# One batch's transposes moved from TensorE to VectorE, and half additions moved forward in the last group

## The chip, the cores and the metric

The kernel runs on one core of a Trainium2 chip. The metric is device time in microseconds (us), the median of three runs. The engines are TensorE (PE, and PEld for its weight loads), VectorE (DVE), ScalarE (ACT), GpSimd (POOL) and SyncE (SP). SP issues most DMAs and does no arithmetic; POOL issues the others. Each engine works through its instructions in the order in which they stand, and waits on semaphores for what the other engines and the DMAs deliver.

## The reference

An attention block on x (4 batches, 8 heads, 512 rows, 64 columns) and a small state (32 rows for each head) feeds two dense layers, one after the other.

```python
scores  = scale * x @ state.T;  a  = softmax(scores);   xread = a @ state
scores2 = scale * state @ x.T;  a2 = softmax(scores2);  sread = a2 @ x
x = concat([xread, sread]) as (4 * 544, 512)
h = x @ w_in;  x = (h - tanh(h)) @ w_out                       # layer 1, 512 -> 2048 -> 512
h = x @ w_in;  out = (h * tanh(softplus(h))) @ w_out           # layer 2, 512 -> 2048 -> 512
```

All of it is float32. Both kinds of scores need x with its 64 columns on the partitions, that is, x transposed.

## The kernel before

A float32 product is made of three passes: each operand is split into a high part (`gh`, `wh`, `ath`) and a remainder (`gl`, `wl`, `atl`), and PE adds high by high, remainder by high and high by remainder. ACT makes the high part, DVE subtracts it for the remainder. The names in the rows are these tiles.

Layer 1 is a sequence of steps, 16 for each batch and 4 for the state rows: steps 0 to 15 are batch 0, 16 to 31 batch 1, 32 to 47 batch 2, 48 to 51 the state rows, 52 to 67 batch 3. A step is an up product into the bank `h` (ACT takes its tanh, DVE subtracts, ACT and DVE split the result into `gh` and `gl`) and, a few steps later, a down product into four banks `acc0` to `acc3`. The four banks are shared by the batches: when a batch ends, ACT and DVE copy them out to `y`, and the next batch's first down product writes them again. Batch 2 begins with `acc3`.

Beside this, each step has side work in a table (`at(step, fn)`): the attention of the next batch, the products `swp` of the state with the weights, and background pieces (`run_piece`) that convert layer 2's weights (`st` tiles, loaded by SP, turned by ACT into `w` and `r`, joined and split by DVE, and stored by POOL as `wi` and `wo`). `keep_pace` decides how many pieces a step runs: it draws straight lines through the points in `pace` and runs pieces while fewer are done than the line says, at most three or four in a step, and only while ten slots of the tile store are free (`RESERVE`).

Batch 2's x is transposed by DVE: `load_xq` brings x in 32 DMAs of 32 KB, in pieces of 128 bytes, so that transposing 32 by 32 blocks (`xt_q`, STREAM_TRANSPOSE) gives what is wanted. The x of the other batches is loaded by `load_x` in rows of 1 KB, transposed by PE in four 128 by 128 products into a side bank (`xtp`), and copied out to `xt`. For batch 3 this stands in the steps 35, 35, 36 and 37, and the scores in step 39. `at_sread` uses the tiles of `load_x` too.

Layer 2 runs in groups of seven products each (a form of Strassen's method). In the last two groups DVE also joins the halves of earlier results into `out` (`combos`: four additions of 256 columns in each of the four items `second(0)`, `second(1)`, `first(0)`, `first(1)`). They wait in the list `soon`, and `slot`, which runs after each of the seven products, takes one item from it. The last group's down products then go through three banks `acc` in turn, and DVE adds each into `out` before the bank is written again.

The lines that order the moved work:

```python
        v = u.t.rearrange("p (i g d) -> p i g d", i=2, g=8)          # load_xq
        V.transpose(out=XT[b, k].t, in_=u.t)                         # xt_q
            if soon and done[0] != 4:                                # slot, in group
                soon.popleft()()
        at(start[b - 1] + (8 if b == QUARTERS else -1), lambda b=b: load_x(b))
    pace = [(start[1] + 8, 0), (start["s"], 52), (start["2"], 96)]
```

All slots of the tile store come from one list (`get`, `put`); `newest` takes the slot that was given back last. The instruction order that results is made by a scheduler, within the dependencies.

Of the kernel before, what the change touches and what calls it, by code (L numbers as in the profile page):

```python
# [31 lines left out]
QUARTERS = 2  # L32
# [48 lines left out]
def attention_moe_kernel(  # L81
# [16 lines left out]
    KD = DM // 128  # L98
# [24 lines left out]
    def get(name, dtype=F32, newest=False, whole=False):  # L123
        if halves and dtype == F32 and not whole:
            return halves.popleft()
        i = free.pop() if newest else free.popleft()
        return Unit(slots.tile([128, 512], dtype, tag=f"k{i}", name=name), i)
# [311 lines left out]
    def load_xq(b, k):  # L439


        u = get("xq", whole=True)
        v = u.t.rearrange("p (i g d) -> p i g d", i=2, g=8)
        for i in range(2):
            src = x[b, 2 * k + i].rearrange("(l g e) (c d) -> (e c) l g d", g=8, e=2, c=2)
            for c in range(4):
                nc.sync.dma_start(out=v[c * 32:(c + 1) * 32, i], in_=src[c])
        P["q", b, k] = u
# [45 lines left out]
    def sc_c(b, i):  # L494
        SC[b, i] = get("scs")
        out = SC[b, i].t.rearrange("p (q e l h) -> p q e l h", q=2, e=2, h=4)
        for e in range(2):
            src = P["c", b][e][:, i * 256:(i + 1) * 256]
            if b == QUARTERS:
                src = src.rearrange("p (h q l) -> p q l h", h=4, q=2)  # L500
            else:
                src = src.rearrange("p (q l h) -> p q l h", q=2, h=4)
            evac(out[:, :, e], src, e if b else 1 - i)
# [127 lines left out]
        )  # L631

    def at_steps(b):
        turn = xt_q if b == QUARTERS else at_xt
        return [lambda k=k: turn(b, k) for k in range(KD)] + [
            lambda: at_scores(b),
            lambda: (at_exp(b, 0), at_exp_t(b, 0)),
            lambda: at_norm(b, 0),
            lambda: (at_exp(b, 1), at_exp_t(b, 1), at_read_t(b, 0)),
            lambda: at_norm(b, 1),  # L640
            lambda: at_read_t(b, 1),
            lambda: at_sread(b),
            lambda: at_sturn(b),
        ]
# [383 lines left out]
        V.tensor_tensor(out=o.t, in0=bank, in1=u.t, op=ALU.add)  # L1028
        return o

    def group(u, g, fill, ahead, with_s, rate, whole=False, keep=0, per=(), mid=None, end=None):


        a, b, c = (psum.tile([128, 512], F32, tag=t, name="h") for t in UB)
        whole_g[0] = g
        done = [0]
        more = rate + (rate > 1)

        def slot(pieces, *after):
            done[0] += 1  # L1040
            for _ in range(2 if done[0] - 1 in per else 1):
                if len(fill) > keep:
                    f = fill.popleft()
                    if f:
                        f()
            if soon and done[0] != 4:
                soon.popleft()()
            for f in after:
                f()
            for _ in range(1 if whole else 2):  # L1050
                if ahead:
                    ahead.popleft()()
            background(pieces, 0)

        def free_w(*xs):
            for x in xs:
                put(*(W2.pop((g, x, k)) for k in range(KH)))

        product(u, g, "m1", a, True)
        m1 = copy_of(a)  # L1060
        slot(more)
        product(u, g, "m6", b, True)
        p = plus(b, m1)
        slot(more)
        product(u, g, "m7", c, True)
        if with_s:
            hs = psum.tile([128, 512], F32, tag=SB_, name="hs")
            gs = s_up(g, hs)
        free_w("a1")
        slot(rate)  # L1070
        product(u, g, "m2", a, False)
        c11 = mish((0, 0), a, whole=whole)
        slot(0, lambda: mish_lo(*c11))
        if with_s:
            divide = s_turn(g, gs, hs)
        product(u, g, "m5", b, False)
        free_w("s12")
        q = plus(b, m1)
        background(1, 0)
        h22 = plus(c, q, q)  # L1080
        c22 = mish((1, 1), h22.t, h22, whole)
        slot(min(u + g, 1), lambda: mish_lo(*c22))
        product(u, g, "m3", b, False)
        free_w("s34")
        h12 = plus(b, m1, m1)
        c12 = mish((0, 1), h12.t, h12, whole)
        slot(rate, lambda: mish_lo(*c12), *([divide] if with_s else []), *([mid] if mid else []))
        product(u, g, "m4", c, False)
        free_w("a2")
        h21 = plus(c, p, p)  # L1090
        c21 = mish((1, 0), h21.t, h21, whole)
        slot(rate, lambda: mish_lo(*c21), *([end] if end else []))
        while len(fill) > keep or ahead:
            slot(rate)
# [84 lines left out]
    soon = deque()  # L1179
# [208 lines left out]
    def at(step, fn, back=None):  # L1388

        def held():  # L1390
            kept = [e.floor for e in engines]
            for e, m in zip(engines, marks[-back]):
                e.floor = m
            fn()
            for e, m in zip(engines, kept):
                e.floor = m

        side.setdefault(step, []).append(held if back else fn)

    seq = []  # L1400
    start = {}
# [27 lines left out]
                at(k + 5, lambda b=b: at_sturn(b), 1)  # L1429
    when = {2: (3, 4, 5, 7, 8, 9, 10, 11, 12, 13, 15, 16), 3: (3, 3, 4, 5, 7, 8, 9, 11, 12, 12, 13, 15)}  # L1430
    for b in (2, 3):
        if b == QUARTERS:
            for k in range(KD):
                at(start[b - 1] + when[b][k] - 3, lambda b=b, k=k: load_xq(b, k))
        at(start[b - 1] + (8 if b == QUARTERS else -1), lambda b=b: load_x(b))
        for i, f in zip(when[b], at_steps(b), strict=True):
            at(start[b - 1] + i, f)
    for b in (1, 2, 3):
        at(start[b] - (3 if b > 1 else 1), lambda b=b: at_a(b))
    at(start[3], lambda: bg.extend(pieces_y(0) + list(late)))  # L1440
    pace = [(start[1] + 8, 0), (start["s"], 52), (start["2"], 96)]
    done = [0]

    def keep_pace(i):
# [146 lines left out]
    for j, (u, g) in enumerate(groups):  # L1591
        n = j % len(ROUND2)
        plain = u == 0 or n >= WHOLE
        ahead = loads_out(g) if plain else deque()
        if j + 1 < len(groups):
            ahead += loads_in(groups[j + 1][1])
        if u and n == 0:
            background(len(bg), 0)
        if (u, n) == (0, 2):
            background(len(bg), 0)  # L1600
            send(now[0] + 1, 0)
            send(0, now[0] + 1)
            widen(stage.tile([128, 1024], F32, tag="st", name="wide") for _ in range(3))
            later = pieces_y(1)
            bg.extend(pieces_ys() + later[:EARLY])
        elif (u, n) == (0, last_g):
            bg.extend(later[EARLY:])
            load, steps = more_t(ROUND2[4])
            ahead.append(load)
        rate = 2 if n == last_g or u == 0 and n < 2 else 1  # L1610
        fill = list(fill)
        if u == 0:
            group(u, g, deque(fill), ahead, False, rate)
            fill = downs(u, g, False)
            continue
        if plain:
            if n == WHOLE:
                fill = deque(fill)
                early, closing = combos(2 * u)
                soon.extend([lambda: None, lambda: None, early])  # L1620
                group(u, g, fill, ahead, True, rate, keep=4, per=(0, 2, 4, 6))
                fill = list(fill) + downs(u, g, True)
            else:
                soon.extend(closing)
                first = fill[4:]
                fill = deque(fill[:4] + first[:2] + first[4:5] + first[2:4] + first[5:])
                group(u, g, fill, ahead, True, rate)
                fill = downs(u, g, True, True)
            continue
        if n == 0:  # L1630
            soon.extend(steps)
            fill = [None] * 2 + fill[:4] + [None] * 3 + fill[4:]
            load, steps = more_t(ROUND2[5])
        elif n == 1:
            ahead.append(load)
        elif n == 2:
            soon.extend(steps)
        pair = ROUND2[n - n % 2:n - n % 2 + 2]
        fill = deque(fill)
        if n % 2:  # L1640
            ahead.extend([lambda i=i, p=pair: load_forms(p, i) for i in range(2)])
            group(
                u, g, fill, ahead, True, rate, True, 0, (), lambda p=pair: prep(p, 0),
                lambda g=g: take_group(g),
            )
            fill = pair_items(pair)
        else:
            group(
                u, g, fill, ahead, True, rate, True, len(fill) - 7, (), None,
                lambda g=g: take_group(g),  # L1650
            )
# [35 lines left out]
```

## Time and profile before

| what | value |
|---|---|
| runs | 701.02, 701.65, 701.98 us, median 701.65 us |
| profiled execution | 700.36 us, of it 698.6 us from its first to its last instruction |
| PE busy | 690.3 us (99%) |
| DVE busy | 514.9 us (74%) |
| ACT busy | 366.0 us (52%) |
| POOL busy | 90.6 us (13%) |
| chain that ended last | PE 42%, issue 37%, POOL 7%, ACT 5%, DVE 4%, DMA 4% |

Busy time is summed over instructions that overlap on PE, and a matmul's end is modelled, so the start of one matmul to the start of the next is the better measure of what it costs. A timeline row gives the start, the length, the engine, the line (nearly all have L68, where a helper records them), what is written and read, how many instructions were merged, and in brackets the idle time of the engine before it and what ended that.

### The profile page before, as it was taken

The numbers are of one execution on the slowest core, as the hardware profiler recorded it, in microseconds if no ns is written. First come the engines' busy times: TensorE is split into PE (matmuls) and PEld (weight loads), VectorE is DVE, ScalarE is ACT, GpSimd is POOL, SyncE is SP. The second block draws the span as 40 slices with busy tenths as digits, with TensorE's granted clock in tenths as the row PEclk, the third lists the DMA queues.
The fourth block names the chain that finished last, engine by engine and source line by source line (L and its number), as shares of the span: only waits on it lengthen the run. The fifth ranks groups of instructions, "written<-read, shape, count | busy, mean of one in ns | idle before, by whom it ended". The sixth has DMA issues, their size and how long they took to land.

```text
span 698.6 us, 11347 instructions
## 1 busy us (share of the span) xinstructions
PE 690.3 (99%) x4166; PEld 564.4 (81%) x4166; DVE 514.9 (74%) x904; ACT 366.0 (52%) x667; POOL 90.6 (13%) x136
## 2 busy tenths in 40 slices
PE   8999999999999999999999999999999999999998
PEld 6467777787777898778888888888888999999976
DVE  5899966796579847998476876767787555776784
ACT  6999644666576757877465432234424463433330
POOL 0000000116022323501222000111011000001000
PEclk9999999999999999999999999999999999999999
DMA  9886221318363677665959643667779676466303
GB/s 293 323 282 231 61 45 18 91 53 272 114 191 139 217 249 246 232 251 154 384 178 306 214 137 105 213 224 225 270 245 307 200 230 196 152 202 220 91 0 136
DMA packets 70952, 134.45 MB, mean 192 GB/s; under 512 B 16880, under 2 KB 27376, under 8 KB 70896
## 3 DMA queue, kind: packets, MB, share of 16 engines
q1 hardware_dynamic: 60656, 100.16, 44.2%
q0 software_dynamic: 10240, 33.56, 13.3%
q8 instruction: 33, 0.54, 0.3%
q14 instruction: 23, 0.19, 0.1%
HBM read 97.78 MB, written 35.91 MB: 191 GB/s over the span
## 4 chain that ended last, share of the span: by engine, by line
PE 42%; issue 37%; POOL 7%; ACT 5%; DVE 4%; DMA 4%; SPq 1%; POOLq 0%; ACTq 0%
PE acc L68 22%; PE h L68 15%; POOL wi L272 4%; POOL wo L272 2%; PE hs L68 2%; ACT r L68 2%; ACT w L68 2%; POOL wt L1149 1%; DMA x<-in_x_dram 1%; DMA wi<-wh 1%; DVE out L68 1%; DMA wide<-in_moe_w_out_dram 1%; PE swp L68 1%; DMA wt<-wl 1%; DVE wide L68 1%
## 5 line engine op out<-in xcount | busy, mean ns | idle before, releaser
L68 PE MATMUL h<-yh,ws 128*128 128x512 f32 x448 | 156.2, 392 | 0.1
L68 PE MATMUL acc<-wo,gh 128*128 128x512 f32 (+1 forms) x332 | 101.4, 387 | 0.4 <-DVE out L68 0.4
L68 PE MATMUL acc<-gh,wh 128*128 128x512 f32 x244 | 98.4, 403 | 0.0
L68 PEld LDWEIGHTS h<-yh,ws 128*128 128x128 f32 x448 | 84.3, 188 | 17.1 <-DVE wide L68 0.7
L68 PE MATMUL acc<-gh,wl 128*128 128x512 f32 x244 | 95.3, 391 | 0.0
L68 PE MATMUL acc<-gl,wh 128*128 128x512 f32 x244 | 95.2, 390 | 0.0
L68 PE MATMUL h<-yl,ws 128*128 128x512 f32 x224 | 87.6, 391 | 0.0
L68 DVE TENSOR_TENSOR gl<-wide,gh 128x512 fp32r<-128x512 f32 x79 | 53.6, 687 | 31.3 <-ACT gh L68 30.7
L68 PEld LDWEIGHTS acc<-wo,gh 128*128 128x128 f32 x332 | 61.9, 188 | 13.3 <-DVE out L68 0.8
L68 PE MATMUL acc<-wf,gh 128*128 128x256 f32 x384 | 70.5, 283 | 0.0
L68 ACT ACTIVATE wide<-wide 128x512 f32<-128x512 f32 x39 | 24.7, 633 | 83.0 <-DVE wide L68 83.0
L68 DVE TENSOR_TENSOR wide<-h,wide 128x512 f32<-128x512 f32 x76 | 52.1, 686 | 17.2 <-ACT wide L68 10.3
L68 PEld LDWEIGHTS acc<-wf,gh 128*128 128x128 f32 x384 | 62.0, 191 | 2.7
L68 PE MATMUL acc<-wo,gl 128*128 128x512 f32 (+1 forms) x166 | 64.2, 387 | 0.0
L68 PEld LDWEIGHTS acc<-gh,wh 128*128 128x128 f32 x244 | 45.8, 188 | 18.2 <-issue 4.2
L68 ACT ACTIVATE wide<-h 128x512 f32<-128x512 f32 x41 | 24.3, 593 | 61.9 <-PE h L68 55.1
L68 PE MATMUL acc<-wf,gl 128*128 128x256 f32 x192 | 54.3, 283 | 0.0
L68 PEld LDWEIGHTS acc<-gh,wl 128*128 128x128 f32 x244 | 45.8, 188 | 10.0
L68 PEld LDWEIGHTS acc<-gl,wh 128*128 128x128 f32 x244 | 45.9, 188 | 9.0 <-issue 0.4
L68 PE MATMUL h<-ath,swh 128*128 128x512 f32 x128 | 51.5, 403 | 1.2 <-ACT swh L68 1.2
L68 ACT ACTIVATE gh<-wide 128x512 fp32r<-128x512 f32 x79 | 48.4, 629 | 7.6 <-DVE wide L68 6.4
L68 PE MATMUL h<-ath,swl 128*128 128x512 f32 x128 | 50.5, 395 | 0.5 <-DVE swl L68 0.5
(220 smaller groups left out, 1289.3 us busy)
## 6 DMA issues: line engine op xcount, KB each, us to landing
ws<-wi SPq DMA_DIRECT2D x128, 256.0 KB, 4.5
st<-in_moe_w_in_dram SPq DMA_DIRECT2D x26, 512.0 KB, 5.4
wo<-wo SPq DMA_DIRECT2D x48, 256.0 KB, 4.1
st<-in_moe_w_out_dram SPq DMA_DIRECT2D x23, 512.0 KB, 5.0
wi<-wh POOLq DMA_DIRECT2D x32, 256.0 KB, 3.9
wi<-wl POOLq DMA_DIRECT2D x32, 256.0 KB, 4.4
wf<-wt SPq DMA_DIRECT2D x24, 256.0 KB, 5.1
wf<-wo SPq DMA_DIRECT2D x24, 256.0 KB, 3.7
```

The costliest lines, as they stand in the source:

```text
L68: i = fn(*args, **kw)
L272: nc.gpsimd.dma_start(out=d, in_=v if len(d.shape) == 2 else v.rearrange("p (g e) -> p g e", g=2))
L1149: nc.gpsimd.dma_start(out=D2T[g][:, 2 * j:2 * j + 2, h, :], in_=u.t.bitcast(F32).rearrange("p (i e) -> p i e", i=2),)
```

## The change

Batch 3's x goes the way of batch 2's: 32 DMAs by SP in step 31 (`start[2] - 1`, all four tiles at once), in slots given back last, and four DVE transposes in the steps in which PE's stood. The tiles of `load_x` for batch 3, which only `at_sread` needs now, are loaded in step 39 in place of step 31. `sc_c` reads the scores of batch 3 in the order that it has for batch 2. `pace` has six points in place of three. In the last group an item of `soon` is taken at the start of the third and of the fourth slot and none at the end of these.

```diff
-        u = get("xq", whole=True)
+        u = get("xq", newest=b > QUARTERS, whole=True)
...
-            if b == QUARTERS:
+            if b >= QUARTERS:
                 src = src.rearrange("p (h q l) -> p q l h", h=4, q=2)
...
-        turn = xt_q if b == QUARTERS else at_xt
+        turn = xt_q if b >= QUARTERS else at_xt
...
+            if soon and sooner and done[0] in (3, 4):
+                soon.popleft()()
             for _ in range(2 if done[0] - 1 in per else 1):
                 if len(fill) > keep:
                     f = fill.popleft()
                     if f:
                         f()
-            if soon and done[0] != 4:
+            if soon and done[0] != 4 and not (sooner and done[0] == 3):
                 soon.popleft()()
...
-        if b == QUARTERS:
-            for k in range(KD):
-                at(start[b - 1] + when[b][k] - 3, lambda b=b, k=k: load_xq(b, k))
-        at(start[b - 1] + (8 if b == QUARTERS else -1), lambda b=b: load_x(b))
+        for k in range(KD):
+            at(
+                start[b - 1] + (when[b][k] - 3 if b == QUARTERS else -1),
+                lambda b=b, k=k: load_xq(b, k),
+            )
+        at(start[b - 1] + (8 if b == QUARTERS else 7), lambda b=b: load_x(b))
...
-    pace = [(start[1] + 8, 0), (start["s"], 52), (start["2"], 96)]
+    pace = [
+        (start[1] + 8, 0), (start[2] + 4, 15), (start["s"] - 4, 28), (start["s"], 38),
+        (start[3], 50), (start["2"], 96),
+    ]
...
-                group(u, g, fill, ahead, True, rate)
+                group(u, g, fill, ahead, True, rate, sooner=True)
```

On PE the order is the same before and after, but for the 16 transposes `xtp`, which are gone. On the other engines it differs in three places that matter here.

The first is SP's queue around batch 3's x. `st` are weights to be converted, each a load into one of three buffers. Before:

```order
L198 DMA st_1131<-in_moe2_w_out_dram 128x1024
L198 DMA st_1559<-in_moe2_w_out_dram 128x1024
L198 DMA st_1785<-in_moe2_w_out_dram 128x1024
L198 DMA st_2038<-in_moe2_w_in_dram 128x1024
L198 DMA st_2047<-in_moe2_w_in_dram 128x1024
```

And after:

```order
L198 DMA st_1131<-in_moe2_w_out_dram 128x1024
L198 DMA st_1559<-in_moe2_w_out_dram 128x1024
L447 DMA xq_2011<-in_x_dram 32x8x32
L198 DMA st_1785<-in_moe2_w_out_dram 128x1024
L447 DMA xq_2011<-in_x_dram 32x8x32 x7
L447 DMA xq_2020<-in_x_dram 32x8x32 x8
L447 DMA xq_2029<-in_x_dram 32x8x32 x8
L447 DMA xq_2038<-in_x_dram 32x8x32 x8
L198 DMA st_2066<-in_moe2_w_in_dram 128x1024
L198 DMA st_2075<-in_moe2_w_in_dram 128x1024
```

The 32 loads of x stand between the weight loads, and 31 of them behind one weight load that has to wait for its buffer.

The second is DVE's order at the end of batch 1, where it copies `acc1` and `acc3` out for batch 2. Before:

```order
L68 TENSOR_TENSOR t_2101<-h_2094,t_2101 128x512
L68 TENSOR_TENSOR gl_2105<-t_2101,gh_2104 128x512
L68 TENSOR_TENSOR wide_72<-h_2132,wide_72 128x512
L68 TENSOR_TENSOR swl_2161<-swp_2146,swh_2159 128x512
L68 TENSOR_TENSOR gl_2142<-wide_72,gh_2141 128x512
L68 TENSOR_TENSOR swl_2157<-swp_2145,swh_2155 128x512
L68 COPY y_2170<-acc1_1314 128x512
L68 COPY y_2180<-acc3_1316 128x512
```

And after:

```order
L68 TENSOR_TENSOR wide_72<-h_2122,wide_72 128x512
L68 TENSOR_TENSOR gl_2132<-wide_72,gh_2131 128x512
L68 SCALAR_TENSOR_TENSOR w_2439<-w_2439,r_2440 128x512
L68 STREAM_TRANSPOSE xt_2218<-xq_2011 128x512
L68 TENSOR_TENSOR wide_72<-h_2153,wide_72 128x512
L68 TENSOR_TENSOR swl_2182<-swp_2167,swh_2180 128x512
L68 TENSOR_TENSOR gl_2163<-wide_72,gh_2162 128x512
L68 TENSOR_TENSOR swl_2178<-swp_2166,swh_2176 128x512
L68 COPY wide_72<-acc1_1314 128x512
L68 COPY y_2200<-acc3_1316 128x512
```

A piece's joining operation and the first of the four transposes have come in ahead of the last subtraction from `h`; the other three transposes stand behind these rows, one for each step.

The third is DVE's order in the last group. Before:

```order
L68 TENSOR_TENSOR wide_4219<-acc_7133,wide_4219 128x512
L68 TENSOR_TENSOR out_7153<-r_5976,r_5672 128x256
L68 TENSOR_TENSOR out_7155<-r_5976,r_5672 128x256
L68 TENSOR_TENSOR out_7153<-r_5976,r_5822 128x256
L68 TENSOR_TENSOR out_7155<-r_5976,r_5822 128x256
L68 TENSOR_TENSOR out_6169<-acc_6828,out_6169 128x512
L68 TENSOR_TENSOR gl_7175<-wide_4221,gh_7166 128x512
L68 TENSOR_TENSOR wide_74<-h_7051,wide_4220 128x512
L68 TENSOR_TENSOR wide_74<-h_7052,wide_74 128x512
L68 TENSOR_TENSOR out_7153<-acc_7190,out_7153 128x512
L68 TENSOR_TENSOR out_7198<-r_6022,wide_4219 128x256
```

And after:

```order
L68 TENSOR_TENSOR out_7151<-r_5995,r_5841 128x256
L68 TENSOR_TENSOR wide_4239<-acc_7155,wide_4239 128x512
L68 TENSOR_TENSOR out_7184<-r_6040,r_5728 128x256
L68 TENSOR_TENSOR out_7186<-r_6040,r_5728 128x256
L68 TENSOR_TENSOR out_7184<-r_6040,wide_73 128x256
L68 TENSOR_TENSOR out_7186<-r_6040,wide_73 128x256
L68 TENSOR_TENSOR out_6187<-acc_6844,out_6187 128x512
L68 TENSOR_TENSOR gl_7197<-wide_72,gh_7182 128x512
L68 TENSOR_TENSOR wide_4239<-h_7067,wide_4237 128x512
L68 TENSOR_TENSOR wide_4239<-h_7068,wide_4239 128x512
L68 TENSOR_TENSOR out_7149<-acc_7212,out_7149 128x512
```

Each of the four items of four additions stands one place of the group earlier: the first before `acc_7155` is added, the second right behind it. The last `gl` of the group, which before stood behind four additions, has none ahead of it now.

## Rows read from the trace of the kernel before

**Rows 1.** The page's busy time, its share of the span and instruction counts

```profile
PE 690.3 (99%) x4166; PEld 564.4 (81%) x4166; DVE 514.9 (74%) x904; ACT 366.0 (52%) x667; POOL 90.6 (13%) x136
```

**Rows 2.** PE's waits: us in total, times, longest

```profile
PE h L68 <- ACT swh L68: 1.2, 2, 1.0
PE acc L68 <- DVE out L68: 0.4, 1, 0.4
```

**Rows 3.** PE's timeline around batch 3's transposes

```profile
181.57 0.39 PE L68 MATMUL h<-ath,swh 128*128 128x512 f32 x1
...
182.70 0.39 PE L68 MATMUL h<-ath,swl 128*128 128x512 f32 x1
182.93 0.60 PE L68 MATMUL xtp<-ident,wide 128*128 128x128 f32 x4
...
183.72 0.47 PE L68 MATMUL acc<-gh,wh 128*128 128x512 f32 x1
184.03 0.40 PE L68 MATMUL acc<-gl,wh 128*128 128x512 f32 x1
...
187.93 0.60 PE L68 MATMUL xtp<-ident,x 128*128 128x128 f32 x4
...
188.60 0.40 PE L68 MATMUL acc<-gl,wh 128*128 128x512 f32 x1
...
192.50 0.60 PE L68 MATMUL xtp<-ident,x 128*128 128x128 f32 x4
...
193.18 0.39 PE L68 MATMUL acc<-gl,wh 128*128 128x512 f32 x1
```

**Rows 4.** The tile xt: duration ns min/median/max, first and last start

```profile
L68 ACT ACTIVATE xt<-xtp x10: 589/596/608, 6.6 to 193.2; 128x512 f32<-128x512 f32 x10
...
L68 DVE STREAM_TRANSPOSE xt<-xq x2: 702/704/706, 106.1 to 115.5; 128x512 f32<-128x512 f32 x2
```

**Rows 5.** The tile xq (batch 2): the same columns, and the landing of its DMAs

```profile
L447 SPq DMA_DIRECT2D xq<-in_x_dram x32: 561/607/803, 87.3 to 108.3; - x32
...
DMA to landing us min/median/max: 2.1/2.4/2.9
```

**Rows 6.** Timelines of DVE, PE, SP and ACT at the end of batch 1

```profile
178.47 0.69 DVE L68 TENSOR_TENSOR wide<-h,wide 128x512 f32<-128x512 f32 x1 [2.05 <-ACT wide L68]
...
181.29 1.28 DVE L68 COPY y<-acc 128x512 f32<-128x512 f32 x2
...
164.04 1.10 PE L68 MATMUL srd<-x,e 128*32 128x64 f32 x64
...
163.81 19.05 SPq L198 DMA_DIRECT2D st<-in_moe_w_out_dram  x3
...
166.36 0.67 ACT L68 ACTIVATE r<-st 128x512 uint32<-128x512 uint32 x1
```

**Rows 7.** Landing of the three x loads in the window 160 to 180

```profile
DMA to landing us min/median/max: 7.1/7.1/7.2
```

**Rows 8.** DVE's timeline in the last group

```profile
663.51 1.42 DVE L68 TENSOR_TENSOR out<-r 128x256 f32<-128x256 f32 x4
665.72 0.69 DVE L68 TENSOR_TENSOR out<-acc,out 128x512 f32<-128x512 f32 x1 [0.79 <-PE acc L68]
...
667.31 1.42 DVE L68 TENSOR_TENSOR wide<-h,wide 128x512 f32<-128x512 f32 x2 [0.31 <-PE h L68]
...
675.89 0.75 DVE L68 TENSOR_TENSOR out<-r 128x256 f32<-128x256 f32 x2
...
677.23 0.68 DVE L68 TENSOR_TENSOR gl<-wide,gh 128x512 fp32r<-128x512 f32 x1
677.83 1.88 DVE L68 TENSOR_TENSOR out<-acc,out 128x512 f32<-128x512 f32 x3
```

**Rows 9.** Timelines of ACT and PE in the last group

```profile
676.07 0.63 ACT L68 ACTIVATE gh<-wide 128x512 fp32r<-128x512 f32 x1
...
677.76 0.39 PE L68 MATMUL acc<-wo,gl 128*128 128x512 f32 x1
678.57 0.73 PE L68 MATMUL acc<-wo,gh 128*128 128x512 f32 x2 [0.41 <-DVE out L68]
679.14 0.40 PE L68 MATMUL acc<-wo,gl 128*128 128x512 f32 x1
```

More of the change, by code (lines that the diff above doesn't have):

```diff
@@ L1029, in plus, with group @@
         return o
-    def group(u, g, fill, ahead, with_s, rate, whole=False, keep=0, per=(), mid=None, end=None):
+    def group(u, g, fill, ahead, with_s, rate, whole=False, keep=0, per=(), mid=None, end=None, sooner=False):
         a, b, c = (psum.tile([128, 512], F32, tag=t, name="h") for t in UB)
```

## The prediction

> **What bounds the kernel now.** I began with the page's busy times. PE is busy for 690.3 of 698.6 us, DVE for 514.9 and ACT for 366.0 [rows 1]: the reader is to see that no engine but PE is near its limit. Then PE's own waits: the largest releaser adds up to 1.2 us, and DVE's `out` to 0.4 us [rows 2]. So almost nothing can be won by waiting less. Time falls if PE has fewer instructions, or if the 0.4 us goes, and it rises if a new wait comes in. That makes three questions: what PE's 16 transposes cost in their place, what DVE and the loads do in the places where the work goes, and what the last group's wait is made of. The timelines of these places answer them, with the durations of the two tiles `xt` and `xq`.
>
> **The 16 transposes on PE.** A plain matmul starts 0.23 us after the one before it (182.70 to 182.93) [rows 3]. The first of eight transposes starts at 182.93, where the first `acc` product would start without them; the second `acc` product would follow at 182.93 + 0.23 = 183.16. It stands at 184.03, so eight transposes cost 0.87 us. Likewise 187.93 + 0.23 = 188.16 against 188.60 is 0.44, and 192.50 + 0.23 = 192.73 against 193.18 is 0.45. Together 0.87 + 0.44 + 0.45 = **1.76 us**, all on the path, since PE has no gap there. PE's order is otherwise unchanged, so this goes in full unless another engine is late.
>
> The row shows 0.60 us for four transposes that overlap, and 0.44 us of PE's time taken by them [rows 3]. The Trainium skill ("TensorE: Matmul & The Clock Gate", Part 4, on the transpose in PE mode) gives some 275 ns for each in one kernel's setting. By that figure 16 would be an estimate of 4.4 us, and the kernel would come out near 697. In this trace they take well under half of that, so the row decides and the figure gets no chance of its own.
>
> **The copies on ACT.** Four ACT copies of `xt`, 0.596 us each, go [rows 4], 2.4 us in all. ACT is busy 52% of the span, and PE's order near them is limited by PE: gain 0. The bounds are 0 and the few hundredths by which a later ACT result comes sooner.
>
> **The transposes on DVE.** Four STREAM_TRANSPOSE of 0.704 us come in, by batch 2's rows [rows 4]: 2.8 us on an engine that is idle for a quarter of the time. The three later ones stand one to a step of 4.57 us (187.93 to 192.50 [rows 3]) and have that idle share for cover. The first stands where DVE is needed, at the end of batch 1. There it moves in, with a joining operation, ahead of a subtraction from `h` that starts at 178.47 after an idle 2.05 us, so DVE is free from 176.42 [rows 6]. The joining operation has the size of that subtraction, 0.69 us; it ends at 177.11, the transpose at 177.81. That leaves 0.66 us of the idle time.
>
> What waits for DVE there is PE's first down product of batch 2. Six products from 181.57 on [rows 3] end at 181.57 + 6 x 0.23, so without the eight transposes PE wants `acc3` at 182.95, where it came to it at 183.72 before. DVE's copies of `acc1` and `acc3` end at 181.29 + 1.28 = 182.57 [rows 6]. The margin falls from 1.15 to about 0.36 us. The transposes were the cover of this copy, and the first place to stall is here: any delay of DVE above 0.66 + 0.36 = 1.02 us is a wait of PE.
>
> **The loads of x.** The 32 issues take SP 0.607 us each (0.561 to 0.803) and land 2.4 us after issue for batch 2 [rows 5]. The first can go when its slot is free, which PE's state product leaves at 164.04 + 1.10 = 165.1. The other 31 stand behind a weight load (`st_1785`) that waits for its buffer. ACT gave that buffer back at 166.36 + 0.67 = 167.0 before [rows 6]; one piece sooner or later moves it, and I put it at 168. SP spends 19.05 us on three of these loads, most of it waiting [rows 6], so there is room for the 32 issues, but not ahead of that wait. The first tile's last piece is then issued at 168.0 + 0.6 + 6 x 0.607 = 172.2 and lands at 174.6 with 2.4 us. DVE wants it at 177.1: in time, by 2.5 us. The nearest row on the other side is the landing of batch 3's `x` by POOL in this stretch, 7.1 us [rows 7], where weight loads lie in the same queues. With that it lands at 179.3, or at 180.5 if each issue takes 0.803; DVE is 2.2 to 3.4 us late, and PE waits for 2.2 - 1.02 = 1.2 to 3.4 - 1.02 = 2.4 us. So this costs 0 to 2.4 us. I take 0.2, since the row of the same shape and size is batch 2's own, and its landing leaves 2.5 us. The last tile's last issue is at 168.6 + 30 x 0.607 = 186.8 and lands by 189.2 to 193.9, against a place at 192.5 and scores two steps later: 0.
>
> The Trainium skill speaks against these loads ("DMA: Bandwidth & Descriptors", on why small descriptors are slow): a piece of memory under 512 bytes doesn't reach the queues' rate, and these are of 128. What batch 2's rows show is 2.4 us for 32 KB with SP issuing one each 0.6 us [rows 5], and so far no wait; by the page's rule a crowded queue would make the landing long, which is the second rival below.
>
> **The other loads, the pace.** `load_x` for batch 3 goes eight steps later; its only reader now is the state product behind the scores, a batch's lead away: 0. The pace changes the count of pieces by at most two at any step and ends at the same point: layer 2's weights come with the same last pieces. No row shows what a piece more or less in a step does; the nearest is the 1.2 us that PE waits for ACT in all its steps [rows 2], and I bound it by half a microsecond either way and take 0.
>
> **The last group.** PE starts a product at 677.76 and the next at 678.57 instead of 677.99, 0.58 us late, and the pair that follows takes 0.57 instead of 0.46, another 0.11 [rows 9]. The wait names DVE's `out` [rows 9], an addition that starts at 677.83 and must free the bank: PE goes on 0.74 us after its start [rows 8, 9]. It starts late because `gl` is made just ahead of it, at 677.23, and ahead of that stand four half additions, of which two are left at 675.89 with 0.75 us [rows 8]. DVE has idle time earlier: 0.79 us before 665.72 and 0.31 before 667.31, and 1.42 us is what four additions take [rows 8]. Each item one place sooner puts the second item into that idle time, and none ahead of the last `gl`. That `gl` then waits for ACT's `gh`, which ends at 676.07 + 0.63 = 676.70 [rows 9]. It starts at about 676.72, 0.51 sooner; the addition moves with it to 677.32, and PE goes on at 677.32 + 0.74 = 678.06, against 678.57. Gain **0.5 us**; the bounds are 0, if `gh` or the addition's place holds it back, and 0.58 + 0.11 = 0.69.
>
> **Sum.** -1.76 - 0.5 + 0.2 = -2.06 on the profiled 700.36 us gives 698.3. The median of the runs, 701.65, stands 1.29 above the profiled execution, so I forecast 701.65 - 2.06 = **699.6**. Its own range is 698.7 (-1.76 - 0.69 - 0.5 for the pace) to 700.4 (-1.76 + 0.5).
>
> **The rivals.** The first: the end doesn't gain. For it speaks that `gl` there depends on ACT as well; against it, that ACT's `gh` ends 0.5 us before `gl` starts. Then -1.76 + 0.2 gives 701.65 - 1.56 = 700.1.
>
> The second: the gain is eaten at the end of batch 1. The pieces land with the 7.1 us of the stretch [rows 7], DVE stops at its first transpose with the whole of `h`'s remainders and the copies of `acc1` and `acc3` behind it, and PE waits for these. With the middle of 1.2 and 2.4, that is -1.76 - 0.5 + 1.8, or 701.2. For it: the row is of this very stretch, and the margin is 0.36. Against it: the change takes these x loads out of the stretch.
>
> The third, slower: SP doesn't get past `st_1785` in time. All but one of the x loads are queued behind it; if the piece that frees its buffer falls one step later, everything moves by 4.57 us, and with a landing of 7.1 us the first tile is there at 183.9, DVE stops for 6.8 us and PE for 6.8 - 1.02 = 5.8. That is +3.5, or 705.2. It decides from a lateness of 1.02 + 2.26 = 3.3 us at the first transpose. For it: SP stands waiting in this stretch, and the order of SP is not chosen by what DVE needs. Against it: the buffer came free at 167.0, and two things must go wrong together.
>
> **Chances.** The forecast 0.58, no gain at the end 0.10, eaten 0.21, slower 0.11. A measurement of this kernel can tell about 0.2%, 1.4 us, from no change: the bound is 700.25. The forecast and the first rival lie below it: 0.68 faster, 0.21 the same, 0.11 slower. The range reaches from 698.5, just under the lower bound of the sum, to 701.9, above the second rival; it leaves out the third and some on either side.
>
> **What would show it.** On PE 4150 matmuls, and `acc` behind `h` with a spacing of 0.23 near 183, 188 and 192. Four more transposes on DVE of 0.70, four copies fewer on ACT. Around 181 to 183 no wait of PE for DVE's `y`, or one of a few tenths; a wait of a microsecond there would be the second rival, and the row before it would be DVE idle for the DMA `xq`. SP's first x loads at 165 to 169, landing in 2 to 3 us. In the last group a wait for `out` of 0.1 us or none. The prediction is wrong if PE shows new waits of over 1 us in steps 31 to 40, or if the last group's wait stays with the products in the same places.

## The result, and the profile after

The changed kernel takes 708.13 us (median of 5 runs, 707.24 to 708.66) against 701.63 us; the ratio is 1.0096, interval 1.0080 to 1.0113. It is slower by 6.5 us, where 2.1 us faster was forecast. The profiled execution took 708.66 us, of it 706.9 us from the first to the last instruction.

The page's busy times after, which answer to [rows 1]:

```profile
PE 691.2 (98%) x4150; PEld 564.4 (80%) x4150; DVE 517.1 (73%) x908; ACT 364.4 (52%) x663; POOL 90.6 (13%) x136
```

PE has the 16 instructions fewer, DVE four more, ACT four fewer, as the change says. PE's busy time does not fall, because a part of it ran at a lower clock. PE's waits after, as in [rows 2]:

```profile
PE h L68 <- DVE wide L68: 5.4, 1, 5.4
PE h L68 <- ACT swh L68: 1.9, 2, 1.7
...
PE acc L68 <- DVE y L68: 0.8, 1, 0.8
```

The first was not there before, and one wait makes all of it. The second is at 34 us, ahead of everything that was moved. The third is at the end of batch 1. The `out` wait of the last group is gone. PE's timeline around the long wait:

```profile
528.87 0.39 PE L68 MATMUL acc<-wo,gl 128*128 128x512 f32 x1
534.64 0.80 PE L68 MATMUL h<-yh,ws 128*128 128x512 f32 x1 [5.38 <-DVE wide L68]
535.23 0.63 PE L68 MATMUL h<-yl,ws 128*128 128x512 f32 x1
...
539.92 0.63 PE L68 MATMUL h<-yh,ws 128*128 128x512 f32 x1
540.35 0.53 PE L68 MATMUL h<-yl,ws 128*128 128x512 f32 x1
540.72 0.61 PE L68 MATMUL h<-yh,ws 128*128 128x512 f32 x2
```

The same three matmuls (the first two and the last of these lines) in the kernel before:

```profile
528.63 0.39 PE L68 MATMUL acc<-wo,gl 128*128 128x512 f32 x1
528.85 0.39 PE L68 MATMUL h<-yh,ws 128*128 128x512 f32 x1
...
532.03 0.61 PE L68 MATMUL h<-yh,ws 128*128 128x512 f32 x2
```

This is layer 2, some 335 us behind the last moved transposes. PE stands for 5.4 us, and then its products are 0.43 us apart (539.92 to 540.35) instead of 0.23. The windows of the same stretch (busy time of PE, PEld, DVE, ACT and POOL, then the granted clock) show the clock that PE had:

```profile
530.00:535.00 5.00, 0.36 (x1) 0.36 (x2) 1.07 (x2) 0.00 (x0) 0.00 (x0) 0.88 0.79 275
535.00:540.00 5.00, 5.00 (x13) 3.84 (x13) 2.29 (x4) 2.82 (x6) 1.45 (x2) 0.50 0.59 176
540.00:545.00 5.00, 5.00 (x28) 4.38 (x27) 4.80 (x9) 0.90 (x2) 0.00 (x0) 0.94 0.80 268
```

Behind the wait the granted clock is 0.50, the lower level of 1.2 GHz. Setting the same matmul of both traces side by side, the changed kernel is 0.24 us late ahead of the wait (528.87 against 528.63), 5.79 us behind it (534.64 against 528.85) and 8.69 us late at 540.72 (against 532.03): 5.55 us at the wait and 2.9 us while the clock was down, 8.45 us in all. What PE waits for is on DVE, and what DVE waits for is on SP. The two timelines there, DVE's and SP's:

```profile
526.90 0.68 DVE L68 TENSOR_TENSOR wl<-tf,wh 128x512 fp32r<-128x512 f32 x1
533.89 1.42 DVE L68 TENSOR_TENSOR wide<-h,wide 128x512 f32<-128x512 f32 x2 [6.31 <-DMA out_dram<-wide]
...
527.01 0.34 SPq L1016 DMA_DIRECT2D out_dram<-wide  x1
```

DVE is to write a sum into a half of a tile `wide`. That half held output rows of batch 0, and the store that SP issued at 527.01 is still reading it. DVE stands until the store is through; until then the bank `h` isn't read, and PE can't write it. The same two places in the kernel before:

```profile
527.69 1.42 DVE L68 TENSOR_TENSOR wide<-h,wide 128x512 f32<-128x512 f32 x2 [0.32 <-PE h L68]
...
525.74 1.40 SPq L1016 DMA_DIRECT2D out_dram<-out  x2
```

There the output lay in a tile `out`, and DVE's sum waited for PE's `h` alone. The work in this stretch is the same in both kernels; what differs is which tile each result was given. `get` takes a half tile if one is free, otherwise the tile that has been free longest, and `put` appends the output's tile as soon as its store is issued. Followed through these lists, the output OUT[0, 1] lay in a whole tile before, which 36 other requests preceded; after, it lies in a half, the list of halves is empty when it is given back, and the fourth request takes it.

The two other moved places: the products that answer to [rows 3], in which the transposes are gone, and DVE in the last group, which answers to [rows 8].

```profile
188.63 0.39 PE L68 MATMUL h<-atl,swh 128*128 128x512 f32 x1
...
189.08 0.39 PE L68 MATMUL acc<-gh,wh 128*128 128x512 f32 x1
189.31 0.39 PE L68 MATMUL acc<-gl,wh 128*128 128x512 f32 x1
```

```profile
685.48 0.69 DVE L68 TENSOR_TENSOR gl<-wide,gh 128x512 fp32r<-128x512 f32 x1 [0.77 <-ACT gh L68]
686.09 1.88 DVE L68 TENSOR_TENSOR out<-acc,out 128x512 f32<-128x512 f32 x3
```

```profile
686.50 0.39 PE L68 MATMUL acc<-wo,gl 128*128 128x512 f32 x1
686.83 0.74 PE L68 MATMUL acc<-wo,gh 128*128 128x512 f32 x2
```

The last `gl` waits for ACT's `gh`, as worked out, and PE's gap behind 686.50 is 0.33 us where it was 0.81 [rows 9].

### The profile page after: what moved, and what is told of

Its sections match the earlier page's. It is cut to its first block, busy times and chain, and to the rows that moved or that the text cites. A ratio compares the mean times of both kernels' runs of the same rounds, so it can differ in the third digit from the quotient of the medians.

```text
span 706.9 us, 11377 instructions
## 1 busy us (share of the span) xinstructions
PE 691.2 (98%) x4150; PEld 564.4 (80%) x4150; DVE 517.1 (73%) x908; ACT 364.4 (52%) x663; POOL 90.6 (13%) x136
## 4 chain that ended last, share of the span: by engine, by line
PE 85%; ACT 5%; DMA 3%; DVE 2%; issue 2%; POOL 1%; SPq 0%; POOLq 0%; DVEq 0%; ACTq 0%
PE acc L68 47%; PE h L68 33%; PE hs L68 2%; ACT r L68 2%; ACT w L68 2%; PE swp L68 2%; POOL wi L272 1%; DMA out_dram<-wide 1%; DMA wide<-in_moe_w_out_dram 1%; DMA x<-in_x_dram 1%; ACT gh L68 1%; PE sct L68 1%; ACT t L68 1%; DMA wi<-wh 0%; PE xtp L68 0%
```

## The experiments

Each kernel was timed beside the kernel before on the same chip (700.64 to 700.79 us). The last column names a wait by the time of the same matmul in the kernel before.

| run | what is different | median us | ratio, interval | PE's new waits of 0.5 us and over |
|---|---|---|---|---|
| a_rest | changed kernel, stored tiles given back later | 699.87 | 0.9979, 0.9964 to 0.9995 | acc at 184: 0.6 |
| no_pace | changed kernel, old pace | 709.34 | 1.0123, 1.0109 to 1.0138 | 221: 3.1; 266: 0.6; 277: 2.9 |
| x31 | changed kernel, load_x in step 31 | 702.37 | 1.0026, 1.0014 to 1.0037 | acc at 184: 1.2; 493: 0.5 |
| t_only | transposes and load_x in step 39 alone | 710.67 | 1.0146, 1.0132 to 1.0161 | 221: 5.2; 277: 2.1; 306: 0.8 |
| b_haz | before, one tile given back first | 708.60 | 1.0116, 1.0102 to 1.0130 | 528: 4.9 |
| p_only | six points of pace alone | 700.78 | 1.0010, 0.9997 to 1.0024 | 493: 0.9 |
| t_x31 | transposes alone, load_x in step 31 | 707.71 | 1.0113, 1.0096 to 1.0131 | acc at 184: 6.0 |
| a_late | a_rest, transposes 1 to 2 steps later | 698.83 | 0.9977, 0.9966 to 0.9988 | acc at 184: 0.6 |
| r_steps | a_rest, x loads tile by tile | 703.41 | 1.0046, 1.0033 to 1.0059 | acc at 184: 2.2 |
| rl_steps | a_late, x loads tile by tile | 701.06 | 1.0008, 0.9997 to 1.0020 | acc at 184: 1.5 |
| rl_28 | a_late, x loads in step 28 | 705.05 | 1.0062, 1.0050 to 1.0074 | acc at 184: 4.4 |
| b_rest | before, stored tiles given back later | 700.94 | 1.0004, 0.9995 to 1.0013 | none |

**The tile that a store still reads: a_rest, b_haz, b_rest.** The first gives a stored tile back when two more have been stored:

```diff
+            resting.append(o)
+            if len(resting) > 2:
+                put(resting.popleft())
+            return
```

> The changed kernel, but a stored output tile goes back to the store of tiles only when two more have been stored, so that the next half tile that is asked for isn't the one that a store is still reading. Theory 1 (DVE waits at 528 us because it was handed the half tile that the store of out_dram is reading, and PE behind it): the 5.4 us wait of PE for DVE's wide and the stretch at half clock behind it (about 2.9 us) both go, 708.1 - 8.4 = 699.7 us, ratio to the kernel before about 0.997; the 0.8 us wait for y at 184 us stays. Rival (the store or the weight loads are late there because the DMA queues are crowded, whatever tile is used): a wait of several us stays at 528 us, 706 us or more.

699.87 us, on the forecast of the theory. The wait at 528 us and the lower clock are both gone, and PE's waits have no row for `wide`. DVE's sum, which now gets a tile `mt`, and the window:

```profile
526.98 0.69 DVE L68 TENSOR_TENSOR mt<-h,wide 128x512 f32<-128x512 f32 x1 [0.33 <-PE h L68]
```

```profile
530.00:535.00 5.00, 5.00 (x29) 4.38 (x28) 4.24 (x8) 2.61 (x6) 1.34 (x2) 1.00 1.04 408
```

The control, the same edit on the kernel before:

> The kernel before with the tiles given back later, and nothing else: the control of a_rest. In the kernel before no output is handed out while PE depends on it (one is, at 536 us, with DVE idle for 1.6 us and PE not waiting), so no change, within 0.5 us of before. If it is faster by 0.5 us or more, that share of what a_rest showed is the edit's own.

No change, so the edit brings nothing of its own. And the other way round, the handing-out put into the kernel before:

```diff
+            if (b, r) == (0, 1):
+                halves.appendleft(o)
+                return
```

> The kernel before, with one edit: the tile of the second output rows of batch 0 (OUT[0, 1]) is given back at the head of the list of half tiles when its store has been issued, so that the same later request takes it as in the changed kernel. Nothing else is moved. Theory 1 (handing out a tile that a store still reads is the whole of the loss): a wait of PE for DVE of about 5.4 us near 527 us and a stretch at half clock behind it, +8.4 us, about 709 us, ratio 1.012. Rival (the wait needs the changed kernel's loads or pieces): within 1 us of before.

708.6 us: the loss appears with nothing moved. Its waits of PE, and DVE's timeline:

```profile
PE h L68 <- DVE out L68: 4.9, 1, 4.9
```

```profile
533.19 0.69 DVE L68 TENSOR_TENSOR out<-h,wide 128x512 f32<-128x512 f32 x1 [5.76 <-DMA out_dram<-out]
```

The wait and the lower clock behind it cost 7.4 us there, 5.0 and 2.4. So one tile that is handed out under its store is enough for the loss, and where no such tile is handed out, in a_rest, the loss at 528 us is gone.

**The parts of the change: p_only, t_only, no_pace, x31, t_x31.** `t_only` has the transposes, with load_x in step 39, without the pace and the half additions, `no_pace` everything but the pace, `p_only` the pace alone; `x31` and `t_x31` put one line back:

```diff
-        at(start[b - 1] + (8 if b == QUARTERS else 7), lambda b=b: load_x(b))
+        at(start[b - 1] + (8 if b == QUARTERS else -1), lambda b=b: load_x(b))
```

> The kernel before with the six points of pace alone. The counts of pieces change by at most three, and only in steps 33 to 37. Theory: no change, within 0.7 us of before. Rival (the points by themselves thin out the pieces where DVE and ACT are full): up to 0.7 us faster by the waits for swh and swl that are there before.

> The changed kernel with the three points of pace of before. Theory 1: by the list of tiles the output of batch 0 that is stored there lies in a whole slot again, which is asked for 36 requests later; no wait at 528 us, 699.5 to 700.5 us. Rival (the transposes' loads of x, which are still all there, are what costs): near 708 us.

> The changed kernel with load_x of batch 3 back in step 31, the six points of pace kept. Theory 1: the list of tiles again puts that output into a whole slot, no wait at 528 us, 699.5 to 701 us (the x loads come back into the stretch where the pieces of 128 bytes land, so the wait for y at 184 us may be up to 1 us longer). Rival (the six points of pace by themselves bring the wait): near 708 us.

> Only the transposes are moved: pace of before, half additions in the last group where they were. Theory 1: no wait at 528 us; the transposes give 1.76 us less what the wait for y at 184 us takes (0 to 0.9), 700.0 to 701.0 us, with the 0.4 us wait for out in the last group still there. Rival (the loads of 128-byte pieces cost the 8 us): near 708 us.

> Only the transposes are moved, pace of before, and load_x of batch 3 stays in step 31. Theory 2 (what cost 9 us with the transposes alone were pieces: load_x in step 39 leaves four tiles free in steps 31 to 38, so that the old pace runs 17, 20, 23, 23, 26, 29 pieces by steps 35 to 40 where it ran 15, 15, 18, 18, 21, 24; here 14, 17, 20, 20, 23, 25): the waits at 221 us shrink to under 2 us, 701 to 704 us. Theory 3 (SP's 32 loads of x push the weight loads behind them late, and ACT waits for these): the loads are all still there, so the waits stay, 708 to 711 us.

`p_only` is no change; but in the kernel before, the six points move the count of pieces by one in steps 33 and 34 and nowhere else, so it says little on them. None of the others has a wait at 528 us, which agrees with the lists: in all of them OUT[0, 1] is a whole tile again. The half comes only when load_x in step 39 and the six points meet. But `no_pace` and `t_only` are as slow as the changed kernel by another way, which I had not foreseen. PE's timeline of t_only, and ACT's before it:

```profile
224.53 1.12 PE L68 MATMUL e2p<-ident,scs 128*128 128x128 f32 x4 [5.15 <-DVE swl L68]
```

```profile
205.15 0.66 ACT L68 ACTIVATE w<-st 128x512 f32<-128x512 f32 x1 [1.84 <-DMA wi<-wh]
...
209.59 0.67 ACT L68 ACTIVATE r<-st 128x512 uint32<-128x512 uint32 x1 [1.67 <-DMA wi<-wl]
...
213.67 0.68 ACT L68 ACTIVATE r<-st 128x512 uint32<-128x512 uint32 x1 [0.62 <-DMA wi<-wl]
...
218.78 0.66 ACT L68 ACTIVATE w<-st 128x512 f32<-128x512 f32 x1 [3.95 <-DMA wi<-wl]
```

ACT stands four times ahead of an instruction that reads a weight tile `st`. The releaser that the profile names is a store by POOL (`wi<-wh`, `wi<-wl`), and it is right: what ACT is to write, `w` or `r`, goes into a tile that this store still reads, as at 528 us. The load that the last of them reads was issued at 201.34 and landed 5.8 us later, at 207.14; the store, by POOL's timeline and its landing:

```profile
213.30 0.72 POOL L272 DMA_DIRECT2D wi<-wl  x1 [0.54 <-DVE wl L68]
...
DMA to landing us min/median/max: 5.3/5.3/5.3
```

It is through at 218.6, and ACT starts at 218.78. The wait at 277 comes about without any weight load: what ACT writes there, `yh`, is made from `wide`.

```profile
283.60 0.63 ACT L68 ACTIVATE yh<-wide 128x512 fp32r<-128x512 f32 x1 [4.52 <-DMA wo<-wl]
```

In no_pace the same `yh` stands for 5.3 us. The kernel gives a converted weight's tile back six pieces after its store was issued, once fewer than 20 tiles are free; the more pieces in a step, the sooner that is. The planner's counts say how it came to this: load_x in step 39 leaves four tiles free in steps 31 to 38, fewer pieces are held back for want of tiles, and the old pace runs 17, 20, 23, 23, 26, 29 by steps 35 to 40, where it ran 15, 15, 18, 18, 21, 24; the six points bring it to 15, 17, 19, 19, 22, 24. So the pace is not an edit beside the transposes, it pays for load_x. `t_x31` bears this out in part: with load_x back, the waits at 221 are gone, as theory 2 had it, but a wait of 6.0 us stands at the end of batch 1, so its time was missed. ACT there:

```profile
175.66 0.66 ACT L68 ACTIVATE w<-st 128x512 f32<-128x512 f32 x1 [4.98 <-DMA wi<-wh]
...
183.02 0.66 ACT L68 ACTIVATE r<-st 128x512 uint32<-128x512 uint32 x1 [2.33 <-DMA wi<-wh]
```

Again ACT stands for POOL's stores: the load that the first reads had landed at 171.96, the store under its `w`, issued at 168.25, was through at 175.59.

In `x31` it is DVE that stands, for the loads of x, of which the first four pieces land 9.0 to 10.1 us after issue:

```profile
178.31 0.71 DVE L68 STREAM_TRANSPOSE xt<-xq 128x512 f32<-128x512 f32 x1 [3.13 <-DMA xq<-in_x_dram]
```

PE's wait is 1.2 us and the time, 702.37 us, is above its forecast: with load_x left in the stretch, the pieces come late in the way of the prediction's second rival. In the changed kernel, without load_x there, the first tile's last seven land in 4.2 to 6.7 us.

**The wait at the end of batch 1: a_late, r_steps, rl_steps, rl_28.** `a_late` moves the transposes behind the copies:

```diff
-    3: (3, 3, 4, 5, 7, 8,
+    3: (4, 5, 5, 6, 7, 8,
```

> The changed kernel with the tiles given back later, as in a_rest, and the four transposes in steps 36, 37, 37 and 38 in place of 35, 35, 36 and 37, behind the copies of acc1 and acc3. Theory 4 (the wait of PE at the end of batch 1, 0.6 to 0.8 us, comes from DVE's first transposes in front of the copies): the wait goes, 699.2 us, 0.6 under a_rest. Rival (it comes from ACT, which stands on a weight load that lands late behind the x loads): the wait stays, 699.9 us.

The wait stays (0.58 us), so the transposes on DVE are not the whole of its cause; but ACT, too, stands longer there than in a_rest (3.7 us for 2.3). 698.83 us is the best time of all, but its interval does not part it from a_rest. In the changed kernel ACT's timeline shows the delay, and POOL's timeline and the landing of its store what ACT stood for:

```profile
177.85 0.67 ACT L68 ACTIVATE w<-st 128x512 f32<-128x512 f32 x1 [2.48 <-DMA wi<-wh]
178.42 0.62 ACT L68 ACTIVATE gh<-wide 128x512 fp32r<-128x512 f32 x1
...
173.32 0.72 POOL L272 DMA_DIRECT2D wi<-wh  x1 [2.42 <-ACT wh L68]
...
DMA to landing us min/median/max: 4.5/4.5/4.5
```

SP issued the load that this `w` reads at 169.12, the loads of x right behind it, and it landed 6.9 us later, at 176.0. The store under `w` was through 1.8 us after that, at 177.8, and ACT starts at 177.85; `gh`, then DVE's chain with the first transpose in it and the copies `y`, are late behind it. Three kernels move the loads of x:

```diff
-                start[b - 1] + (when[b][k] - 3 if b == QUARTERS else -1),
+                start[b - 1] + when[b][k] - 3,                              # r_steps, rl_steps
+                start[b - 1] + (when[b][k] - 3 if b == QUARTERS else -4),   # rl_28
```

> The changed kernel with tiles given back later (as a_rest), and the loads of x issued tile by tile in steps 32, 32, 33 and 34, as for batch 2, in place of all in step 31. Theory 3 (the x loads issued right behind the weight loads share the queues with them, these land after 8 us in place of 4, and ACT, which stands on one of them for 2.3 us, delays the copies of acc1 and acc3): ACT's wait goes, PE's wait at the end of batch 1 falls from 0.6 to 0.2 us or less, 699.4 us. Rival (with the transposes gone there, the chain of DVE and ACT at the batch's end is too long in any case): 0.6 us stays, 699.9 us. A third outcome: the x now lands too late for the first transposes, and PE waits 1 us or more, 700.5 us or more.

> a_late with the loads of x issued tile by tile in steps 33, 34, 34 and 35. Theory 3: the wait at the end of batch 1 goes, 698.4 us (a_late 698.8 less 0.4). Rival: as a_late, 698.8 us.

> a_late with all loads of x issued in step 28 in place of 31; by the counts there are then up to three pieces fewer in steps 28 to 33. Theory 3: the x loads are through before the weight loads of steps 31 to 34, so these land in 4 to 5 us and the wait at the end of batch 1 goes, 698.4 us. Rival: as a_late, 698.8 us.

In all three the wait grows, to 2.2, 1.5 and 4.4 us, against both theories. In each ACT still stands ahead of the copies (2.5, 5.0 and 2.4 us), and each time a store by POOL under the tile that ACT is to write is the last to land. In `r_steps` the third outcome came true beside it: the first transpose waits for its loads, between the two copies:

```profile
183.61 0.71 DVE L68 STREAM_TRANSPOSE xt<-xq 128x512 f32<-128x512 f32 x1 [0.99 <-DMA xq<-in_x_dram]
```

So what the waits of ACT have in common is read from the traces. No run shows it by an experiment: a kernel that gives the weights' tiles back later was not tried, and how much the loads of x in the same stretch lengthen the stores is not settled. No placement that was tried is free of the wait.

## Why the prediction was wrong

**The transposes, -1.76: right.** By matching matmuls, t_only, which has no wait there, gains 0.88, 0.45 and 0.45 us at the three places, 1.78 in all.

**The last group, -0.5: right.** The changed kernel's delay falls by 0.48 us there (8.74 to 8.26), a_rest's by 0.48 too, t_only's, without the edit, by nothing.

**The end of batch 1, +0.2: mis-sized, and by another mechanism.** In the changed kernel the 0.87 us of the first eight transposes turn into 0.16 us lost: the term is 1.03 us, inside its bounds of 0 to 2.4. The prediction looked for DVE idle for `xq`. The first transpose runs at 180.28 without a wait, but partly by luck: its last piece landed at 178.9, 4.2 us after its issue at 174.65, where the prediction had 174.6, 2.4 and 172.2, and DVE came to it so late only because ACT was late. ACT stood for a store by POOL that still read the tile of its `w`. The sum has a term for DVE's transposes and for the landing of x, and none for ACT.

**"The other loads, the pace": this step failed.** It gave both edits 0, the pace with half a microsecond either way, because the counts of pieces change by two and the load has a batch's lead. It looked at when work is done and never at which tile it is given. load_x later and the six points together change the order in which tiles come back, 335 us on that order hands DVE a tile under a store, and this costs 8.45 us, 5.55 of them in the wait. Without it, a_rest comes near the forecast, 0.9979 against 699.6 / 701.65 = 0.9971, which its interval holds; its profiled execution gains 1.1 us of the 2.06, since the end of batch 1 eats the whole gain of the first place.

**Of the rivals** none was it. The third, slower, had the right sign and near the right size, by SP held at a weight load; no run shows that shape. The second is what x31 has in small, with load_x left where it was; the change takes it out, as the prediction argued. The chance of 0.11 for slower was too low for a change that shifts every later allocation.

**The ledger of the profiled executions:** 1.0 us late by 35 us, where nothing was moved (the wait for `swh`); +0.16 at 184, -0.45 and -0.45 at 188 and 192; +8.45 at 528; -0.48 at the end; with small drifts, +8.3.

## What to carry to other kernels

When tiles come from one list, an edit that changes how many are held or in what order they return moves every later allocation: follow each tile that a DMA is still reading to its next writer, in the kernel after, before calling an edit free. A tile under a store belongs at the far end of the list, which costs a few lines here. When an edit makes room (four tiles here), ask which throttled work will use it: the pieces did, and ACT stood for their stores. And when the releaser that a profile names looks wrong for what an instruction reads, look at what it writes.

## What was not expected of the hardware

This stall of PE cost half as much again: 5.55 us at the wait, and 2.9 us more at a granted clock of 0.50 until about 540.6 us. Behind r_steps' wait of 2.2 us the clock fell too (0.66 on average from 185 to 190), behind rl_steps' 1.5 us it didn't (1.00). The windows of these two, r_steps first:

```profile
185.00:190.00 5.00, 4.96 (x15) 3.96 (x16) 3.08 (x5) 2.13 (x4) 2.38 (x4) 0.66 0.54 166
```

```profile
185.00:190.00 5.00, 5.00 (x24) 4.11 (x23) 4.93 (x9) 4.68 (x9) 1.12 (x2) 1.00 0.83 259
```

And a store of 256 KB that is issued in 0.34 us held its tile for up to 6.9 us (527.01 to DVE's start at 533.89); SP had issued four weight loads in the 4 us before it and one right behind. POOL's weight stores of the same size, where ACT stood for them, took from 4.5 us (changed kernel, 173.32) to 7.3 us (t_x31, 168.25).
